# Reordering the last gate writes and the early gathers of a two-stage mixture-of-experts kernel

## Chip, cores and metric

One core of one Trainium2 chip. The metric is device time in microseconds (us) of one execution; lower is better. The kernel before was run three times: 889.64, 891.00 and 892.84 us, median 891.0 us.

## What is computed

Three layers in a row, on 3072 tokens of width 384:

```
attn:  state = w_t * state + k_t v_t ;  y_t = r_t (state + u k_t v_t)       (8 heads of 48)
moe1:  x = ((a @ w1) * (a @ w2)) @ w3 @ w_out                             (384 -> 1024 -> 384)
moe2:  noisy = x @ w_gate + log(1 + exp(x @ w_noise)) * noise              (8 experts)
       top 2 of 8, softmax weights over the two
       out += weight * (relu(x @ w1[e]) @ w2[e])    for the rows of each expert e
```

The last layer is sparse: each token goes to two of eight experts. The tokens of an expert have to be gathered, multiplied and added back to their rows of the output.

## The kernel before, in words

**Stages.** Up to about 452 us the kernel works through 24 tiles of 128 tokens, in 12 groups of two (`g`, 0 to 11). A group has 12 sub-slots (`i`, 0 to 11), and a hand-written list (`at(slot, ...)`, slot = 12 * g + i) says what is added behind which sub-slot. After the groups the eight experts run one after the other.

**Gate.** For a batch of tiles, `gate_top` (line 628) is a generator whose steps are called one at a time between other work: softplus noise, top 2, counting, expert weights (`weights`, lines 678 to 683, from the exponential of line 676), and slot numbers (lines 707 to 722). A slot is a token's place in its expert's list. `gate_put` (line 737) then writes (token, weight) pairs into the table `slots` in DRAM, 128 at a time, by an indirect DMA issued on GpSimd (POOL), line 742. The batches are of four tiles, but the last two are of two: tiles 20 and 21 (`t0` = 20), and tiles 22 and 23 (`t0` = 22), whose x is ready last. The last batch is gated while expert 0's first half already multiplies.

**An expert.** Its list has 7 tiles: 4 (`TA`) of 128 rows in the first half, 2 of 128 and one of 32 in the second (numbers 4, 5 and 6; `NT` = 7). For each tile: the index list is read from the table (SP queue, line 828 for the first experts, line 818 later), the rows of x are gathered by an indirect DMA on POOL (line 836 or 867), stored as a compact block in DRAM (SP, line 841 or 873), and read back turned by a DMA transpose into `XTx` (SP, line 848 or 879). ScalarE and VectorE split it into a high and a low part (lines 884 and 885), and TensorE multiplies: `mm1` (line 891) for eight blocks `ff` of the hidden layer, each read out by ScalarE (line 900) and VectorE (line 901), then `mm2` (line 905) for each tile, with the result scattered to the output by POOL (line 928).

**Order.** SP's DMAs are all kept in program order, and each waits in the queue for its own semaphores. VectorE, TensorE and, from the last group on, ScalarE run in program order (manual schedule); the order on POOL is that of the scheduler unless an instruction is pinned with `keep_in_program_order`. For expert 0 some gathers start before all of x or all slots are there: tile 3 (`TA` - 1) needs the slots of `t0` = 16, tile 4 (`TA`) those of `t0` = 20, and tiles 5 and 6 those of `t0` = 22. Expert 1's first half is gathered early too (lines 1037 to 1039).

**Around the change.** Behind the last group, lines 1053 to 1076 issue in this order: gate steps and `mm1(0, ff)` interleaved; in `ff` = 2 the index read of tile 4, its gather, and the turning of expert 1's first half; behind the loop the store of tile 4 (line 1067), the four writes of the last gate batch (line 1070), the turning of tile 4 (line 1073), then index reads and gathers of tiles 5 and 6 (lines 1074 to 1076), and `mm2(0, 0)` to `mm2(0, 3)`, with the stores and the turning of tiles 5 and 6 issued behind the first of them and the split `tr(0, 1)` behind the third. Expert 0's second half, `mm1(1, ff)`, follows at line 1093 and reads tiles 4 to 6 together.

Of the kernel before, what the change touches and what calls it, by code (L numbers as in the profile page):

```python
# [18 lines left out]
P = 128  # L19
# [3 lines left out]
NCH = N // P  # L23
# [8 lines left out]
TA, TB = 4, 2  # L32
# [4 lines left out]
DUMP = NT * P  # L37
# [34 lines left out]
def tile_kernel(ctx: ExitStack, tc: tile.TileContext, dt, nat, w3t, wout, w1, w2, e1, e2, cf, ci, out):  # L72
    nc = tc.nc
    pe, act, dve, pool, sp = nc.tensor, nc.scalar, nc.vector, nc.gpsimd, nc.sync
# [18 lines left out]
    x2d = nc.dram_tensor("x2_rows", [NROW, 2 * DM], U16, kind="Internal").ap()  # L93
# [376 lines left out]
    def run_todo(lo, hi):  # L470
        for slot in sorted(x for x in todo if lo <= x < hi):
            for fn, a in todo.pop(slot):
                fn(*a)
# [28 lines left out]
    for i, fn in enumerate(STEPS):  # L502
        for j in range(NCH):
            late = 3 if j == NCH - 1 and i == 1 else 0
# [93 lines left out]
    def low_p():  # L598

        while LOWP:  # L600
            l, p, h = LOWP.pop()
            dve.tensor_tensor(out=l, in0=p, in1=f(h), op=OP.subtract)

    def mo_x(g, fp):
        for tt in range(2):
            for fi in range(2):
                ff = 2 * fp + fi
                s = slice(256 * fi + P * tt, 256 * fi + P * tt + P)
                wh, wl = [W0[i][:, ff] if ff < 4 else W1[ff - 4][:, i] for i in range(2)]
                mm3(bX[tt][:, :XW], PH[g, fp][:, s], PL[g, fp][:, s], wh, wl, ff == 0, ff == 7)  # L610

    def mo_lz(g):
        for tt in range(2):
            dve.tensor_copy(out=LZ[:, 2 * g + tt, :], in_=bX[tt][:, DM:XW])

    def mo_out(g, tts=(0, 1), pin=lambda x: x):
        for tt in tts:
            t = 2 * g + tt
            xo = xos[:, 2 * DM * tt:2 * DM * tt + 2 * DM]
            pin(act.copy(out=halves(xo), in_=bX[tt][:, :DM].bitcast(U16).rearrange("p (d t) -> p t d", t=2)))  # L620
            act.dma_start(out=x2d[DUMP + t * P:DUMP + P + t * P], in_=xo)


    GB = 4
# [112 lines left out]
    def gate_put(t0, i, k):  # L737
        si, sf, SC = GT[t0]

        if t0 + GB < NCH:  # L740
            dve.tensor_copy(out=si[:, i, k:k + 1], in_=sf[:, i, k:k + 1])  # L741
        ins = pool.indirect_dma_start(out=table, out_offset=bass.IndirectOffsetOnAxis(ap=si[:, i, k:k + 1], axis=0),  # L742
                                      in_=SC[:, i, k, :], in_offset=None)
        for p in PUT:
            tc.declare_no_dep(ins.ins, p, reason="every slot is given once")
        PUT.append(ins.ins)

    def fill_table():
# [19 lines left out]
    TI, XG, RW, HM, Hh, Hl, XT = {}, {}, {}, {}, {}, {}, {}  # L768
    EP = {}

    def open_a():
        EP["a"] = ctx.enter_context(tc.tile_pool(name="epa", bufs=1))
        for hf in range(2):
            for k in "hl":
                XT[k, hf] = EP["a"].tile([P, 3, NAB[hf]], F32R, name=f"XT{k}{hf}")
        XT["x", 0] = EP["a"].tile([P, 3, NAB[0]], F32, name="XTx0")
        open_h(EP["a"], 0)
# [15 lines left out]
    def load_e(e, m, i):  # L793
        if m == 0 and e:
            rw = EP["b"].tile([P, 1536], F32, name="raww", bufs=2)
        else:
            rw = rawp.tile([P, 1538], F32, name="raw2", tag="raw64")[:, :1536]
        RW[e, m, i] = rw
        tc.keep_in_program_order(sp.dma_start(out=rw, in_=(e1, e2)[m][e, :, 1536 * i:1536 * i + 1536]))
# [31 lines left out]
    def gather_first(j, nch, e=0):  # L831
        if j < TA - 1 and not e:
            XG[e, j] = xgs[:, 2 * DM * (j % 2):2 * DM * (j % 2) + 2 * DM]
        else:
            XG[e, j] = EP["a"].tile([P, 2 * DM], U16, name="xg", bufs=NXG)
        pool.indirect_dma_start(out=XG[e, j][:rows_of(j)], out_offset=None, in_=x2d[:DUMP + nch * P],
                                in_offset=bass.IndirectOffsetOnAxis(ap=ti(e, j)[:, 0:1], axis=0))

    def store_first(j, e=0):
        w = rows_of(j)  # L840
        tc.keep_in_program_order(sp.dma_start(
            out=rows[e, 2 * TPT * j:2 * TPT * j + 2 * w].rearrange("(p t) d -> p (t d)", t=2), in_=XG[e, j][:w]))
# [15 lines left out]
    def rows_of(j):  # L858
        return TPT if j < NT - 1 else TPL

    def ti(e, j):
        hf, jj = divmod(j, TA)
        return TF[:rows_of(j), j] if e == 0 and first else TI[e, hf][:rows_of(j), jj]
# [111 lines left out]
    def gate_at(o, t0, per, put, n=GB):  # L975
        gen = gate_top(t0, n)
        for i in range(11):
            at(o + (per[i] if isinstance(per, tuple) else i // per), next, gen, None)
        for i in range(2 * n):
            at(o - o % SPG + put[i], gate_put, t0, i // 2, i % 2)  # L980


    for t0 in range(0, NCH - GB, GB):
        late = t0 == NCH - 2 * GB
        gate_at(SPG * ((t0 + GB) // 2) + 3, t0, 1 + late,
                tuple(range(8, 8 + 2 * GB)) if late else (13, 14, 17, 17, 19, 20, 23, 23))
    gate_at(SPG * (NGRP - 1) + 3, NCH - GB, (0, 0, 1, 1, 2, 3, 4, 5, 7, 7, 7), (10,) * GB, GB // 2)
    at(SPG + 2, fill_table)
    for i in range(10):
# [5 lines left out]
    for g in range(NGRP):  # L995
        if g == 2:
            ctx.enter_context(tc.manual_schedule(engines={mybir.EngineType.PE}))
        if g == NGRP - 1:
            ctx.enter_context(tc.manual_schedule(engines={mybir.EngineType.Activation}))
        sub = [(mo_ab, g, 0, 0), (mo_ab, g, 0, 1), None, (mo_ab, g, 1, 0), (mo_ab, g, 1, 1), (mo_x, g, 0),  # L1000
               (mo_ab, g, 2, 0), (mo_ab, g, 2, 1), (mo_x, g, 1), (mo_ab, g, 3, 0), (mo_ab, g, 3, 1), (mo_x, g, 2)]
        if g == 0:
            sub[:5] = [(mo_ab, g, 0, 0, bST[0]), (mo_ab, g, 1, 0, bST[1]), None, (mo_ab, g, 0, 1, bA), (mo_ab, g, 1, 1)]
        if g == NGRP - 1:
            cvx.close()
            attx.close()
            sub[8:] = [(mo_ab, g, 3, 0, PB[4]), (mo_ab, g, 3, 1, PB[5]), (mo_x, g, 1), (mo_x, g, 2)]
            open_a()
            load_e(0, 0, 0)
            load_e(0, 0, 1)  # L1010
        for i in range(12):
            if sub[i]:
                act.on = g == 0 and i < 9
                fn, *a = sub[i]
                fn(*a)
            elif g:
                mo_x(g - 1, 3)
                mo_lz(g - 1)
                mo_out(g - 1)
            k = SPG * g + i  # L1020
            run_todo(k - .5, k)
            if i not in (1, 4, 7, 10 if g < NGRP - 1 else 9):
                low_p()
            run_todo(k, k + .5)
            act.on = False
            if g == NGRP - 1:
                if i in (0, 4, 8, 10):
                    split_e(0, 0, (0, 4, 8, 10).index(i))
                if i == 10:
                    load_e(0, 1, 1)  # L1030
                if i == 0:
                    turn_first(0, TPT * (TA - 1))
                if i == 3:
                    index_first(TA - 1, 1)
                    gather_first(TA - 1, NCH - GB)
                    store_first(TA - 1)
                    index_first(0, TA, 1)
                if 4 <= i < 8:
                    gather_first(i - 4, NCH - GB, 1)
                if 5 <= i < 8:  # L1040
                    tr_first(0, TA - 1, (i - 5,))
                if i == 7:
                    turn_first(TA - 1, TPT * TA)
                    load_e(0, 1, 0)
                    for j in range(TA):
                        store_first(j, 1)
# [6 lines left out]
    t0 = NCH - GB // 2  # L1053
    gen = gate_top(t0, GB // 2)
    for ff in range(8):
        for _ in range((5, 1, 1, 0, 0)[ff] if ff < 5 else 1):
            next(gen, None)
        if ff == 0:
            mo_out(NGRP - 1, (1,), tc.keep_in_program_order)
        mm1(0, ff, (bA, bB, PB[4], PB[5]), lambda: ff == 2 and [next(gen, None) for _ in range(2)])  # L1060
        if ff == 2:
            index_first(TA, 1)
            gather_first(TA, NCH - GB // 2)
            turn_first(0, TPT * TA, 1)
        if ff >= 4:
            split_e(0, 1, ff - 4)
    store_first(TA)
    for i in range(GB // 2):
        for k in range(2):
            gate_put(t0, i, k)  # L1070
    movx.close()
    open_b()
    turn_first(TA, TPT * (TA + 1))
# [156 lines left out]
```

## Time and profile before

| | |
|---|---|
| runs | 889.64, 891.00, 892.84 us; median 891.0 |
| profiled execution | 891.74 us, of which the traced span is 889.9 us |
| TensorE matmul busy | 869.9 us (98% of the span), 7333 instructions |
| VectorE, ScalarE, GpSimd busy | 495.1, 434.6, 243.3 us |
| mean granted TensorE clock | 0.994 of full speed |
| chain that ended last | TensorE 85%, VectorE 7%, ScalarE 3%, DMA 1% |

The span is what the trace covers; the time of the execution has 1.8 us more around it. Busy shares are averages over stages: that TensorE is busy 98% says that there are few gaps, and the question is where the remaining ones lie and what ends them. In the rows below, a time in the first column is the start in us from the span's start, the next the duration; `x3` means that several were merged; a bracket gives the idle time of the engine ahead of the instruction and what ended it. `SPq` rows are DMAs being issued on the queue of SP.

### The profile page before, as it was taken

What the parts mean: (1) busy time and instruction counts of PE and PEld (TensorE: products, weight loads), DVE (VectorE), ACT (ScalarE), POOL (GpSimd) and SP (SyncE); (2) the same over time, 40 slices, a digit from 0 to 9 for tenths busy, and PEclk for the clock granted to TensorE, in tenths of its full rate; (3) what the DMA queues carried; (4) which work ended last, traced back from release to release, by engine and by line L of the source; (5) the groups of instructions that cost most, each with busy time, mean ns of one, the idle gap of its engine ahead of it and who ended that gap; (6) DMA issues with size and microseconds to landing.
All of it is one profiled execution on the core that took longest, in us unless ns stands there. A gap on an engine that the chain in (4) does not pass through costs nothing.

```text
span 889.9 us, 18271 instructions
## 1 busy us (share of the span) xinstructions
PE 869.9 (98%) x7333; PEld 809.6 (91%) x7333; DVE 495.1 (56%) x1215; ACT 434.6 (49%) x876; POOL 243.3 (27%) x216
## 2 busy tenths in 40 slices
PE   9999999999999999999999999999999999999994
PEld 6789899999999999999988989899998989999894
DVE  6899866857666667665563453443434344353320
ACT  5777566555556646644553343433344343434320
POOL 2000010131231231232343534316061341603022
PEclk9999999999999999999999999999999999999998
DMA  9964398474574654525173797929276593934113
GB/s 352 406 224 163 113 130 258 125 199 154 140 225 137 188 137 125 151 49 171 37 196 82 207 238 196 207 81 221 62 224 141 137 207 83 225 78 110 18 22 38
DMA packets 123967, 139.22 MB, mean 156 GB/s; under 512 B 74976, under 2 KB 103648, under 8 KB 123872
## 3 DMA queue, kind: packets, MB, share of 16 engines
q1 hardware_dynamic: 100336, 109.58, 43.2%
q0 software_dynamic: 12160, 19.72, 11.7%
q10 hardware_dynamic: 11376, 8.65, 3.0%
q8 instruction: 59, 0.97, 0.5%
q14 instruction: 36, 0.29, 0.1%
HBM read 88.12 MB, written 36.04 MB: 140 GB/s over the span
## 4 chain that ended last, share of the span: by engine, by line
PE 85%; DVE 7%; ACT 3%; issue 2%; DMA 1%; POOL 0%; SPq 0%; POOLq 0%; ACTq 0%; DVEq 0%
PE pb L182 25%; PE pb L183 25%; PE pb L184 25%; PE pb L332 3%; PE pb L263 3%; PE pb L923 1%; PE pb L296 1%; DVE cvz L166 1%; ACT top L153 1%; DVE am L268 1%; PE pb L520 1%; PE pb L412 1%; DVE fg L210 1%; DVE w3l L173 0%; DVE WAl L173 0%
## 5 line engine op out<-in xcount | busy, mean ns | idle before, releaser
L928 POOL DMA_INDIRECT out<-ye,ti x49 | 77.7, 1585 | 225.7 <-ACT ye L918 205.2
L182 PE MATMUL pb<-XTh,WAh 128*128 128x512 f32 (+1 forms) x384 | 132.5, 345 | 1.6 <-ACT XTh L884 1.6
L184 PE MATMUL pb<-XTh,WAl 128*128 128x512 f32 (+1 forms) x384 | 132.1, 344 | 0.0
L183 PE MATMUL pb<-XTl,WAh 128*128 128x512 f32 (+1 forms) x384 | 131.8, 343 | 0.1
L901 DVE SCALAR_TENSOR_TENSOR HH<-pb,HH 128x256 fp32r<-128x256 f32 (+1 forms) x128 | 71.0, 557 | 105.6 <-ACT HH L900 101.3
L182 PE MATMUL pb<-WBh,HH 128*128 128x384 f32 x384 | 129.3, 337 | 0.0
L183 PE MATMUL pb<-WBl,HH 128*128 128x384 f32 x384 | 128.5, 335 | 0.0
L184 PE MATMUL pb<-WBh,HH 128*128 128x384 f32 x384 | 128.4, 334 | 0.0
L900 ACT ACTIVATE HH<-pb 128x256 fp32r<-128x256 f32 (+1 forms) x128 | 62.7, 492 | 109.9 <-PE pb L184 105.3
L918 ACT ACTIVATE ye<-pb,ti 128x384 f32<-128x384 f32 x42 | 24.4, 582 | 130.3 <-PE pb L184 101.8
L742 POOL DMA_INDIRECT slots<-g_sc,g_si x48 | 51.8, 1078 | 125.4 <-DVE g_si L741 73.1
L183 PE MATMUL pb<-xl,WAh 128*128 128x256 f32 x288 | 80.9, 281 | 0.8 <-DVE xl L339 0.8
L182 PE MATMUL pb<-xh,WAh 128*128 128x256 f32 x288 | 81.5, 284 | 0.0
L182 PEld LDWEIGHTS pb<-XTh,WAh 128*128 128x128 f32 x384 | 72.7, 189 | 9.7 <-ACT XTh L884 1.9
L183 PE MATMUL pb<-xl,WBh 128*128 128x256 f32 x288 | 81.0, 281 | 0.0
L182 PE MATMUL pb<-xh,WBh 128*128 128x256 f32 x288 | 81.0, 281 | 0.0
L184 PE MATMUL pb<-xh,WBl 128*128 128x256 f32 x288 | 81.0, 281 | 0.0
L184 PE MATMUL pb<-xh,WAl 128*128 128x256 f32 x288 | 80.8, 281 | 0.0
L183 PEld LDWEIGHTS pb<-XTl,WAh 128*128 128x128 f32 x384 | 73.0, 190 | 7.9 <-DVE XTl L885 0.3
L184 PEld LDWEIGHTS pb<-XTh,WAl 128*128 128x128 f32 x384 | 72.8, 190 | 7.6
L182 PEld LDWEIGHTS pb<-WBh,HH 128*128 128x128 f32 x384 | 72.1, 188 | 5.0 <-ACT WAh L806 3.8
L243 POOL TENSOR_TENSOR rku<-nrk 128x384 f32<-128x384 f32 x21 | 21.6, 1031 | 194.5 <-DVE cc L250 78.9
(203 smaller groups left out, 2064.4 us busy)
## 6 DMA issues: line engine op xcount, KB each, us to landing
dtc<-dt SPq DMA_DIRECT2D x24, 772.0 KB
raw<-e SPq DMA_DIRECT2D x18, 768.0 KB
raww<-e SPq DMA_DIRECT2D x14, 768.0 KB
nrk<-nat SPq DMA_DIRECT2D x24, 384.0 KB
expert_rows<-xg SPq DMA_DIRECT2D x45, 192.0 KB
rawf<-w3t SPq DMA_DIRECT2D x16, 512.0 KB
nv<-nat SPq DMA_DIRECT2D x24, 256.0 KB
out<-zeros SPq DMA_DIRECT2D x9, 576.0 KB
```

The source lines that it names most:

```text
L153: act.activation(out=t.bitcast(F16).rearrange("p (n t) -> p n t", t=2)[:, :, 1], in_=top, func=AF.Copy)
L182: pin(pe.matmul(o, wh, xh, start=start, stop=False))
L183: pe.matmul(o, wh, xl, start=False, stop=False)
L184: pe.matmul(o, wl, xh, start=False, stop=stop)
L243: on.tensor_tensor(out=t, in0=RK[j][:, :DM], in1=RK[j][:, DM:], op=OP.mult)
L263: pe.matmul(bST[hb][:, P * a:P * a + P], KT[j][q, a].rearrange("p s i -> p (s i)"), RT[j][q, a].rearrange("p s i -> p (s i)"), start=True, ...
L332: pe.matmul(o, lt, rh, start=st, stop=en, tile_position=tp)
L742: ins = pool.indirect_dma_start(out=table, out_offset=bass.IndirectOffsetOnAxis(ap=si[:, i, k:k + 1], axis=0), in_=SC[:, i, k, :], in_offs ...
L900: act.activation(out=Hh[hf][:, ff], in_=bank[:, :n], func=AF.Relu)
L901: dve.scalar_tensor_tensor(Hl[hf][:, ff], bank[:, :n], 0.0, f(Hh[hf][:, ff]), op0=OP.max, op1=OP.subtract)
L918: act.activation(out=y[:n], in_=bank[:n], func=AF.Copy, scale=wt)
L928: ins = pool.indirect_dma_start(out=out, out_offset=bass.IndirectOffsetOnAxis(ap=ti(e, j)[:, 0:1], axis=0), in_=y[:n], in_offset=None, com ...
```

## The change

It does four things. The last gate batch: the two generator steps with the exponential and the weights are called ahead of `mm1(0, 0)` in place of ahead of `mm1(0, 1)` and `mm1(0, 2)`, and so ahead of the first block's read-out on ScalarE and VectorE. Its four slot writes are issued ahead of tile 4's gather on POOL, and both are pinned there, as are the gathers of tiles 5 and 6; tile 4's gather and store move behind the writes. The last four slot writes of `t0` = 16 are issued in sub-slots 0, 0, 1, 1 of the last group in place of 0, 1, 2, 3. The index reads of tile 3 and of expert 1, tile 3's gather and store move from sub-slot 3 to 1 of the last group, and expert 1's four gathers from sub-slots 4 to 7 to sub-slots 2 to 5.

```diff
@@ gate_put
             tc.declare_no_dep(ins.ins, p, reason="every slot is given once")
+        if t0 + GB > NCH:
+            tc.keep_in_program_order(ins)
         PUT.append(ins.ins)
@@ gather_first
-        pool.indirect_dma_start(out=XG[e, j][:rows_of(j)], out_offset=None, in_=x2d[:DUMP + nch * P],
-                                in_offset=bass.IndirectOffsetOnAxis(ap=ti(e, j)[:, 0:1], axis=0))
+        ins = pool.indirect_dma_start(out=XG[e, j][:rows_of(j)], out_offset=None, in_=x2d[:DUMP + nch * P],
+                                      in_offset=bass.IndirectOffsetOnAxis(ap=ti(e, j)[:, 0:1], axis=0))
+        if j >= TA:
+            tc.keep_in_program_order(ins)
@@ the list of slots
-                tuple(range(8, 8 + 2 * GB)) if late else (13, 14, 17, 17, 19, 20, 23, 23))
+                (8, 9, 10, 11, 12, 12, 13, 13) if late else (13, 14, 17, 17, 19, 20, 23, 23))
@@ the last group
-                if i == 3:
+                if i == 1:
                     index_first(TA - 1, 1)
                     gather_first(TA - 1, NCH - GB)
                     store_first(TA - 1)
                     index_first(0, TA, 1)
-                if 4 <= i < 8:
-                    gather_first(i - 4, NCH - GB, 1)
+                if 2 <= i < 6:
+                    gather_first(i - 2, NCH - GB, 1)
@@ behind the last group
     for ff in range(8):
-        for _ in range((5, 1, 1, 0, 0)[ff] if ff < 5 else 1):
+        for _ in range(7 if ff == 0 else ff > 4):
             next(gen, None)
...
         if ff == 2:
             index_first(TA, 1)
-            gather_first(TA, NCH - GB // 2)
             turn_first(0, TPT * TA, 1)
         if ff >= 4:
             split_e(0, 1, ff - 4)
-    store_first(TA)
     for i in range(GB // 2):
         for k in range(2):
             gate_put(t0, i, k)
+    gather_first(TA, NCH - GB // 2)
+    store_first(TA)
     movx.close()
     open_b()
     turn_first(TA, TPT * (TA + 1))
```

## Rows read from the trace of the kernel before

**Rows 1.** Timeline of TensorE, 486 to 494 us: around its longest wait.

```profile
486.93 0.34 PE L184 MATMUL pb<-WBh,HH 128*128 128x384 f32 x1
488.87 0.40 PE L182 MATMUL pb<-XTh,WAh 128*128 128x288 f32 x1 [1.60 <-ACT XTh L884]
489.36 0.40 PE L183 MATMUL pb<-XTl,WAh 128*128 128x288 f32 x1
...
490.18 0.44 PE L182 MATMUL pb<-XTh,WAh 128*128 128x288 f32 x1
...
493.30 0.37 PE L183 MATMUL pb<-XTl,WAh 128*128 128x288 f32 x1
```

**Rows 2.** Busy time of each engine by stretch, then PEclk, DMA share, GB/s.

```profile
491.00:492.00 1.00, 1.00 (x6) 1.00 (x5) 0.44 (x2) 0.38 (x1) 0.79 (x1) 0.50 1.00 399
```

**Rows 3.** Waits of TensorE, 440 to 520 us (all there are): total, times, longest.

```profile
PE pb L182 <- ACT XTh L884: 1.6, 1, 1.6
PE pb L727 <- DVE g_rb L714: 0.2, 1, 0.2
```

**Rows 4.** Timeline of SP's DMA queue, 469 to 487 us.

```profile
469.06 0.35 SPq L841 DMA_DIRECT2D expert_rows<-xg  x1
471.35 1.21 SPq L848 DMA_TRANSPOSE XTx<-expert_rows  x1
476.28 0.81 SPq L828 DMA_DIRECT2D tf<-slots  x2
482.32 1.02 SPq L841 DMA_DIRECT2D expert_rows<-xg  x2
484.94 2.09 SPq L848 DMA_TRANSPOSE XTx<-expert_rows  x1
```

**Rows 5.** Waits of SP's queue, 455 to 500 us: total, times, longest.

```profile
SPq L828 <- DMA slots<-g_sc,g_si: 10.8, 2, 7.2
```

**Rows 6.** Timeline of POOL, 465 to 481 us.

```profile
465.38 0.97 POOL L836 DMA_INDIRECT xg<-x_rows,tf  x1 [8.86 <-issue]
466.66 1.55 POOL L742 DMA_INDIRECT slots<-g_sc,g_si  x1 [0.30 <-DVE HH L901]
...
469.78 1.71 POOL L742 DMA_INDIRECT slots<-g_sc,g_si  x1 [0.30 <-issue]
471.79 1.16 POOL L742 DMA_INDIRECT slots<-g_sc,g_si  x1 [0.30 <-issue]
479.28 0.98 POOL L836 DMA_INDIRECT xg<-x_rows,tf  x1 [6.33 <-DMA tf<-slots]
```

**Rows 7.** Timeline of ScalarE, 458 to 462 us.

```profile
458.44 0.80 ACT L620 COPY xos<-pb 128x768 uint16<-128x768 uint16 x1
...
459.65 0.60 ACT L900 ACTIVATE HH<-pb 128x512 fp32r<-128x512 f32 x1 [0.40 <-PE pb L695]
461.07 0.20 ACT L676 ACTIVATE g_d<-g_d 128x2 f32<-128x2 f32 x1 [0.82 <-DVE g_d L675]
```

**Rows 8.** Timeline of VectorE, 459 to 467 us.

```profile
459.19 0.36 DVE L669 TENSOR_TENSOR g_cm<-g_cm,g_mb 128x8 bf16<-128x8 bf16 x2
460.28 0.69 DVE L901 SCALAR_TENSOR_TENSOR HH<-pb,HH 128x512 fp32r<-128x512 f32 x1 [0.72 <-ACT HH L900]
...
463.21 0.16 DVE L707 TENSOR_TENSOR g_ct<-pb,g_gap 128x8 f32<-128x8 f32 x1
...
464.54 0.17 DVE L722 CAST g_si<-g_sf 128x4 int32<-128x4 f32 x1
464.62 1.88 DVE L901 SCALAR_TENSOR_TENSOR HH<-pb,HH 128x512 fp32r<-128x512 f32 x3
```

**Rows 9.** Timeline of TensorE: the first matmul of the fifth block.

```profile
461.61 0.39 PE L182 MATMUL pb<-XTh,WAh 128*128 128x512 f32 x1
```

**Rows 10.** Slot writes, line 742: ns min/median/max; the page's group with their mean.

```profile
L742 POOL DMA_INDIRECT slots<-g_sc,g_si x48: 952/995/1705, 175.8 to 471.8; - x48
L742 POOL DMA_INDIRECT slots<-g_sc,g_si x48 | 51.8, 1078 | 125.4 <-DVE g_si L741 73.1
```

## The prediction

> **What bounds the kernel now.** TensorE is almost never idle, so I first looked for the places where it is. In the stretch that the change touches, its timeline shows one long gap [rows 1]: the last matmul of expert 0's first half starts at 486.93, the next one, the first of the second half, at 488.87 after 1.60 us of waiting for the split of `XTx`, and the second of the half again waits, 0.49 behind the first. Then TensorE is slow: from 490.18 to 493.30, 13 matmuls of 0.24 us, and the stretch in between has a granted clock of 0.50 [rows 2], that is 1.2 in place of 2.4 GHz. What TensorE did before the clock fell was to wait. So this place costs 1.60 of idle, 0.37 of the second matmul (0.49 less 0.12, half of 0.24), and 1.56 (half of 3.12) of slow clock: 3.5 us. The list of TensorE's waits from 440 to 520 holds one more entry, 0.2 us for the gate [rows 3]. Nothing else there can be won.
>
> What the 1.60 us wait for is followed back along SP's queue [rows 4]: the turning of tiles 5 and 6 at 484.94, their stores at 482.32, and at 476.28 the reads of their index lists. From that issue to TensorE's restart at 488.87 it takes 12.6 us. The index read waits for the slot writes to land (the longest such wait is 7.2 us [rows 5]), and the last of them leaves POOL at 472.95. On POOL [rows 6] the four writes run from 466.66, behind tile 4's gather at 465.38, which had stood idle for 8.86 us for its own index list. So the change cuts at the right chain. The question is what holds the index read when the writes no longer do.
>
> **The last weights ahead of the first read-out.** In program order ScalarE now meets the exponential of the gate before its copy of x (line 620) and before the read-outs. Before, the copy began at 458.44, and the exponential, of 0.20, came behind the first read-out [rows 7]. The exponential needs VectorE's step behind the counts, which end at 459.55 [rows 8]; with 0.16 for that step, as for the gate's like ones, it ends near 459.9. So the copy now starts about 1.4 later, and all that is queued behind it does too: the write of x to DRAM (read first by the gather of tiles 5 and 6, some 18 us later, so worth nothing) and the first block's read-out, which followed the copy by 1.21 (459.65) and now comes near 461.1. VectorE's part follows 0.63 behind (460.28) and takes 0.69, so the first block's bank is free near 462.4. The fifth block uses the same bank and began at 461.61 [rows 9]: a new wait of 0.8 us. Against it the gate's matmul need no longer wait its 0.2 [rows 3]. TensorE is 0.6 late at the end of the first half, and the gap at 487 hides that, as it is 1.97 long; without that cover it would cost 0.6.
>
> The slot numbers: the second read-out on VectorE now ends near 462.9, and the last steps (463.21 to 464.71 before) begin there, so they are ready at 464.4 instead of 464.71, and the first write starts at 464.7, with POOL's gap of 0.30, instead of 466.66 [rows 6].
>
> **The writes ahead of tile 4's gather.** The writes come 2.0 us sooner. But the gather of tile 4 now comes behind them, and behind it on SP stand, in order, its store, its turning, and only then the index reads of tiles 5 and 6. Before, store and turning were issued at 469.06 and 471.35 [rows 4], while the writes were still going out, and were free. Now they are in the chain. Its sum, with d for a slot write's time on POOL:
>
> - first write at 464.7, four writes of d + 0.30;
> - tile 4's gather, 0.97 on POOL; from its end to the store's issue 2.06 (480.26 to 482.32, quiet) or 2.71 (466.35 to 469.06, with expert 1's turning beside it). I take 2.06, since that turning is now earlier;
> - store to turning 2.29 (469.06 to 471.35), turning 1.21 to issue; then the index read.
>
> That is 472.4 + 4d. The median write takes 0.995, the shortest 0.952, the longest 1.705, the mean 1.078 [rows 10]. Of the last four, three took 1.55, 1.71 and 1.16 [rows 6], so I take the mean, not the median: index read at 476.74, against 476.28. The shortest gives 476.2, the longest 479.2, and 2.71 in place of 2.06 adds 0.65. A gain larger than 0.1 is excluded as long as SP's queue keeps its order. The landing of the writes is no longer what comes last: the last leaves POOL near 470, and even the 3.33 us that the index read stood behind the last write before end at 473.3.
>
> **Weighed against a rule.** The gather at 465.38 took 0.97, hardly the shortest time, although VectorE ran read-outs with two tensor inputs beside it from 464.62 [rows 8]. The Trainium skill, page GPSIMD Engine Reference, section Specifications, says that GpSimd shares its SBUF interface with VectorE and contends with VectorE's instructions of two SBUF inputs. By that rule all four writes would be long, since VectorE's read-outs and splits now fall on each of them; by the row they need not be. The long case is a rival below, with its price from the rows.
>
> **Early gathers.** Two index reads, five gathers and a store move two sub-slots up on SP and POOL, with two VectorE casts of the `t0` = 16 writes. TensorE waits for none of this before or after [rows 3], and in program order they pass nothing else on either queue. Worth nothing by itself; if the cover is gone the bound is below 0.2, the only other wait. It clears DMA work of expert 1 out of the way of the last writes, which is why I took 2.06. Tile 4's index also comes sooner, but its gather is now behind the writes anyway. The pins cost no instruction.
>
> **Sum.** The index read is 0.5 later, and so are the gathers, stores, turning and TensorE's restart, each of which only hangs on it. TensorE itself is 0.6 late, so its wait is about as long as before, and I leave the slow clock stretch as it is. Profiled execution: 891.74 + 0.5 = 892.2. That execution stands 0.7 above the median of the runs, 891.0, so in terms of the median: 891.5. A measurement of this kernel tells 0.3% (2.7 us) from no change.
>
> **Rivals.** Times in terms of the median.
>
> - The wait goes: the index read follows the writes' landing near 473.3, three us sooner, and everything is there before TensorE. It gains 3.5 and pays 0.6: 888.1, faster by 0.33%. For it: the writes do come sooner. Against: this needs SP to pass tile 4's turning, and its rows stand in program order, each behind its wait. Chance 0.10.
> - Slower: VectorE holds up the slot writes. At d = 1.705 the index read comes at 479.2 and the time is 894.0; over 0.3% it decides from d = 1.63. For it: two of the last four were that long. Against: the gather of 0.97, the mean. Chance 0.17.
> - The clock does not fall, as the wait is split between 462 and 488: 1.56 less, 889.9. Against: the long wait hardly shrinks. Chance 0.08.
> - The change doesn't do what it says: the scheduler's order on POOL leaves gather or scatter ahead of the writes, and the index read is as before: 891.0. The pins speak against it. Chance 0.05.
> - The forecast, 891.5: 0.60.
>
> **How the numbers follow.** Range: from the shortest chain with the slow clock gone, 891.0 - 1.6 = 889.4, to the longest writes, 894.0; outside lie the first rival and the second with the late landing, together under 0.2. Faster by over 0.3%: most of the first rival and a little scatter, 0.08. Slower: most of the second and of its sum with a longer slow stretch, 0.16. Within: 0.76.
>
> **What would show it.** Right: the slot writes start near 464.7; tile 4's gather behind them near 470; SP's index reads directly behind the turning of tile 4, near 476.7, with no wait for slots; a wait of 0.8 before the fifth block; a wait of 1.5 to 2 and a slow stretch near 488. Wrong: an index read by 474, no wait ahead of the second half, no stretch of 0.50 clock; or slot writes of 1.6 each; or a new TensorE wait elsewhere.

## The result, and the profile after

The changed kernel takes 898.58 us (median of 6 runs, 896.29 to 899.71); the kernel before, run beside it, 891.92 (6 runs, 889.64 to 895.82). The ratio on record is 1.0069, with a 95% interval of [1.0042, 1.0097] (here and below it is not the quotient of the two medians): slower, by more than the 0.3% of which the prediction speaks, and outside the range of the forecast.

The profiled execution of the changed kernel took 898.66 us, 6.92 more than that of before. The page shows a TensorE that works hardly longer (871.4 us of matmul in place of 869.9) in a span 7.0 longer: most of the time went into waiting.

```profile
PE 871.4 (97%) x7333; PEld 811.1 (90%) x7333; DVE 496.2 (55%) x1215; ACT 434.1 (48%) x876; POOL 241.7 (27%) x216
```

TensorE's waits of the changed kernel from 440 to 520 us (total, times, longest), against [rows 3]:

```profile
PE pb L182 <- ACT XTh L888: 6.5, 1, 6.5
```

The 0.2 for the gate is gone as predicted, no new wait has come between 455 and 489, and the one wait ahead of expert 0's second half has grown from 1.60 to 6.46. To see where the 6.92 us are, I mark two instructions in each execution: expert 0's first matmul (A), and the first matmul of its second half (R). TensorE's timeline, changed kernel, answering to [rows 1]:

```profile
455.75 0.39 PE L182 MATMUL pb<-XTh,WAh 128*128 128x512 f32 x1
...
488.95 0.34 PE L184 MATMUL pb<-WBh,HH 128*128 128x384 f32 x1
495.74 0.61 PE L182 MATMUL pb<-XTh,WAh 128*128 128x288 f32 x1 [6.46 <-ACT XTh L888]
```

and, kernel before, the one row that [rows 1] does not hold:

```profile
452.88 0.39 PE L182 MATMUL pb<-XTh,WAh 128*128 128x512 f32 x1
```

- Up to A: 455.75 against 452.88, 2.87 later. The change issues hardly anything there, and the next two fences show where more than half of it comes from.
- From A to R: 39.99 against 35.99 us, 4.00 more. This is the change.
- From R to the end of the span: 401.12 against 401.08. Nothing.

The first part shows how a difference of two profiles can mislead. Matched matmul by matmul, the changed kernel is 1.2 us behind at 22 us and 2.8 behind at 40. The busy time by stretch (length; TensorE, weight load, VectorE, ScalarE, POOL with their instructions; granted clock, DMA share, GB/s) from 28 to 36 us, ahead of everything that was changed, before:

```profile
28.00:36.00 8.00, 7.00 (x44) 6.15 (x45) 7.57 (x19) 6.03 (x15) 0.00 (x0) 1.00 1.02 409
```

and changed:

```profile
28.00:36.00 8.00, 6.83 (x33) 6.03 (x33) 7.48 (x18) 5.06 (x11) 0.00 (x0) 0.79 1.02 409
```

The same code ran at a granted clock of 0.79 there: 33 matmuls were done in place of 44. In a second profile of the same changed kernel, told of below, this stretch has 1.00 again and A lies at 453.22. A second profile of the kernel before has A at 453.19. So the 2.87 of the 6.92 is this execution's chance, while the 4.00 from A to R is there again (41.18 against 35.99).

SP's queue in the changed kernel, answering to [rows 4]:

```profile
465.06 0.34 SPq L830 DMA_DIRECT2D tf<-slots  x1
477.48 0.35 SPq L845 DMA_DIRECT2D expert_rows<-xg  x1
479.41 1.22 SPq L852 DMA_TRANSPOSE XTx<-expert_rows  x1
480.80 0.92 SPq L830 DMA_DIRECT2D tf<-slots  x2
487.18 2.05 SPq L845 DMA_DIRECT2D expert_rows<-xg  x2
492.04 1.26 SPq L852 DMA_TRANSPOSE XTx<-expert_rows  x1
```

Store, turning, and the index read directly behind it: the order that the prediction named. POOL, answering to [rows 6]:

```profile
467.54 0.96 POOL L742 DMA_INDIRECT slots<-g_sc,g_si  x1 [8.30 <-DMA tf<-slots]
...
471.33 1.71 POOL L742 DMA_INDIRECT slots<-g_sc,g_si  x1 [0.30 <-issue]
473.34 1.18 POOL L838 DMA_INDIRECT xg<-x_rows,tf  x1 [0.30 <-issue]
483.71 0.96 POOL L838 DMA_INDIRECT xg<-x_rows,tf  x1 [9.19 <-DMA tf<-slots]
484.97 0.87 POOL L838 DMA_INDIRECT xg<-x_rows,tf  x1 [0.31 <-issue]
486.15 1.66 POOL L932 DMA_INDIRECT out<-ye,tf  x1 [0.30 <-issue]
488.12 1.59 POOL L932 DMA_INDIRECT out<-ye,tf  x1 [0.30 <-issue]
```

Two things are new. The first slot write waits 8.30 us for `tf<-slots`, the landing of tile 4's index read, and not for VectorE. And behind the gathers of tiles 5 and 6 stand two scatters of the first half's results, where before there was one. The chain of waits (start, length, what) runs through them:

```profile
484.97 3.90 DMA xg<-x_rows,tf
...
488.88 3.10 DMA expert_rows<-xg
...
492.04 3.19 DMA XTx<-expert_rows
```

Before, the store of the last tile took 1.89, and the turning 3.43:

```profile
482.99 1.89 DMA expert_rows<-xg
...
484.94 3.43 DMA XTx<-expert_rows
```

### The profile page after: what moved, and what is told of

It is laid out like the page before. It is cut to its first block, busy times and chain, and to the rows that moved or that the text cites. A ratio compares the mean times of both kernels' runs of the same rounds, so it can differ in the third digit from the quotient of the medians.

```text
span 896.9 us, 18270 instructions
## 1 busy us (share of the span) xinstructions
PE 871.4 (97%) x7333; PEld 811.1 (90%) x7333; DVE 496.2 (55%) x1215; ACT 434.1 (48%) x876; POOL 241.7 (27%) x216
## 4 chain that ended last, share of the span: by engine, by line
PE 83%; DVE 6%; DMA 4%; issue 2%; ACT 2%; POOL 2%; SPq 0%; POOLq 0%; DVEq 0%; ACTq 0%
PE pb L182 25%; PE pb L183 24%; PE pb L184 24%; PE pb L332 3%; PE pb L263 3%; DMA xg<-x_rows,tf 1%; PE pb L927 1%; PE pb L296 1%; DVE cvz L166 1%; POOL slots L742 1%; DMA slots<-g_sc,g_si 1%; DMA rawf<-wout 1%; DMA expert_rows<-xg 1%; POOL xg L838 1%; ACT top L153 0%
## 5 line engine op out<-in xcount | busy, mean ns | idle before, releaser
L905 DVE SCALAR_TENSOR_TENSOR HH<-pb,HH 128x256 fp32r<-128x256 f32 (+1 forms) x128 | 71.1, 557 | 104.4 <-ACT HH L904 99.5
```

The lines of the kernel that those rows point to most:

```text
L905: dve.scalar_tensor_tensor(Hl[hf][:, ff], bank[:, :n], 0.0, f(Hh[hf][:, ff]), op0=OP.max, op1=OP.subtract)
```

## The experiments

Three theories were set against each other. **A, the place in the queue:** tile 4's gather, store and turning now stand between the slot writes and the index reads of tiles 5 and 6, and that alone makes the wait. **B, the other parts:** the early weights, or the early gathers of expert 1, cost the time. **C, the collision:** since the chain is late, the scatters of the first half meet the last gathers and stores on the DMA engines and stretch them. "Wait" is the wait ahead of the second half in the one profiled execution of each kernel.

**1. The place alone, undone and done.** The changed kernel with only tile 4's gather and store put back ahead of the writes:

```diff
         if ff == 2:
             index_first(TA, 1)
+            gather_first(TA, NCH - GB // 2)
...
+    store_first(TA)
     for i in range(GB // 2):
         for k in range(2):
             gate_put(t0, i, k)
-    gather_first(TA, NCH - GB // 2)
-    store_first(TA)
```

> The changed kernel, but with tile 4's gather and store back ahead of the last four slot writes; early weights, early gathers and pins stay. Theory A (tile 4's store and turning now stand on SP's queue ahead of the index reads of tiles 5 and 6, behind a gather that comes later): TensorE's wait ahead of the second half falls from 6.5 to 2 us or less, and from the first matmul of expert 0 to the first one of its second half it takes 35 to 36.3 us (36.0 before, 40.0 after); ratio to the kernel before 0.997 to 1.002. Rival B (the early weights and the early gathers cost the time): the wait stays over 4 us, the stretch near 40, the ratio near 1.007.

Measured: 891.09 us against 892.85; 0.9997 [0.9973, 1.0022]. The wait is 3.52 and A to R 37.05, more than A's figures, which I had taken from the one profile of before. The profiled execution was one of the slower ones of this kernel (892.86, ninth of 12).

The kernel before with only that move and the pins of the diff:

```diff
-            gather_first(TA, NCH - GB // 2)
...
-    store_first(TA)
     for i in range(GB // 2):
         for k in range(2):
             gate_put(t0, i, k)
+    gather_first(TA, NCH - GB // 2)
+    store_first(TA)
```

> The kernel before, with only tile 4's gather and store moved behind the last four slot writes (and the pins). Theory A: the wait is 5 to 7 us, the stretch from expert 0's first matmul to its second half 39 to 40.5 us, ratio 1.004 to 1.009. Rival B: the wait stays near 1.6, the stretch near 36, the ratio 0.998 to 1.002.

Measured: 896.72 against 892.85; 1.0046 [1.0021, 1.0071]. The wait, 9.04, and A to R, 42.57, are more than A's figures. TensorE's timeline:

```profile
496.20 0.61 PE L182 MATMUL pb<-XTh,WAh 128*128 128x288 f32 x1 [9.04 <-ACT XTh L888]
```

The whole loss goes with this one move: undone, the kernel is where before is; done alone, it is slow. B is left with little.

**2. The other parts by themselves.** The early weights alone:

```diff
-        for _ in range((5, 1, 1, 0, 0)[ff] if ff < 5 else 1):
+        for _ in range(7 if ff == 0 else ff > 4):
```

> The kernel before, with only the early weights (all seven gate steps ahead of the first block's multiplication). Theory A: nothing to gain or lose, as the slot writes stand behind tile 4's gather; ratio 0.998 to 1.002, the wait ahead of the second half 1.5 to 4 us as in the runs with the order of before, and no new wait of TensorE ahead of the fifth block. The step of the prediction (a new wait of 0.8 us near the fifth block) would show as a second TensorE wait of 0.5 to 0.9 us. Rival B: ratio 1.003 or more.

Measured: 1.0009 [0.9985, 1.0033], wait 3.65, and no second wait of TensorE. The early gathers alone (the new list of slots, `i == 1`, `2 <= i < 6`):

> The kernel before, with only the earlier slot writes of tiles 16 to 19 and the earlier index reads and gathers in the last group. Theory A: tile 4's index read comes up to 2 us sooner, counted from expert 0's first matmul; the time is within 0.997 to 1.001. Rival B: ratio 1.003 or more, with a wait over 4 us.

Measured: 0.9982 [0.9957, 1.0006], wait 4.12; tile 4's index read came 2.2 us sooner after A (7.60 in place of 9.76; 8.98 in the second profile of before). Both intervals hold 1: B has fallen. Both waits are above the 1.60 of before, but each belongs to its own execution: those profiled took 895.90 and 894.38, among the slowest of their kernels, with medians of 894.05 and 891.11.

**3. The queue place without giving up the early writes.** If A is right, the index reads and gathers of tiles 5 and 6 need only go ahead of tile 4's store and turning on SP:

```diff
     gather_first(TA, NCH - GB // 2)
+    for j in (NT - 2, NT - 1):
+        index_first(j, 1)
+        gather_first(j, NCH)
     store_first(TA)
     movx.close()
     open_b()
     turn_first(TA, TPT * (TA + 1))
-    for j in (NT - 2, NT - 1):
-        index_first(j, 1)
-        gather_first(j, NCH)
```

> The changed kernel, with the index reads and gathers of tiles 5 and 6 issued ahead of the store and the turning of tile 4 on SP. Theory A: the index read waits for the slot writes alone and comes some 3 to 4 us sooner than in the changed kernel, the wait falls to 0 to 2.5 us, the stretch to 34 to 36.5; ratio 0.996 to 1.001. Rival B: the wait stays over 4 us, ratio near 1.007. Theory C (the two scatters ahead of the stores are what costs most): the wait falls by less than 2 us.

Measured: 889.35 against 892.85; 0.9974 [0.9953, 0.9995]: faster than before, and, by the ratios, 0.9974 against 1.0069 and (experiment 5) 1.0054, 0.8% to 0.9% faster than the changed kernel. SP's queue shows the index read 20.2 us behind A (453.24 here), where the changed kernel has 25.05:

```profile
473.40 0.81 SPq L830 DMA_DIRECT2D tf<-slots  x2
476.24 0.36 SPq L845 DMA_DIRECT2D expert_rows<-xg  x1
478.23 1.23 SPq L852 DMA_TRANSPOSE XTx<-expert_rows  x1
```

and TensorE waits 1.45:

```profile
488.22 0.40 PE L182 MATMUL pb<-XTh,WAh 128*128 128x288 f32 x1 [1.45 <-ACT XTh L888]
```

**4. The scatters.** The changed kernel, with the scatters of the first half held back and issued behind the gathers of expert 1's second half (line 928 before):

```diff
+        if HELD is None: scatter()
+        else: HELD.append(scatter)
...
     need(1, 1, 0)
+    with tc.issue_after(GL[0]):
+        for fn in held: fn()
```

> The changed kernel, with the scatters of expert 0's first half issued on POOL behind the gathers of expert 1's second half, so that none runs beside the gathers and stores of tiles 5 and 6. Theory C (the two scatters that now run there slow the gather, the store and the turning): the turning of tiles 5 and 6 follows its stores by 2 us in place of 3.1, and the wait falls from 6.5 to 3.5 to 4.5 us; ratio 1.002 to 1.005. Theory A alone (place in the queue, without collision): the wait stays at 6 us or more, ratio 1.006 to 1.008.

Measured: 895.45 against 892.85; 1.0028 [1.0006, 1.0051], wait 4.12 in place of 6.46. Its chain of waits:

```profile
482.80 2.50 DMA xg<-x_rows,tf
...
485.31 2.46 DMA expert_rows<-xg
...
487.84 3.40 DMA XTx<-expert_rows
```

The three legs of the last tile (gather to store, store to turning, turning to landing) are 8.4 us here and 10.2 in the changed kernel. So C is a part of the loss: 0.28% is left of the 0.69% and (experiment 5) 0.54%, which is about half, and the intervals are too wide to say it closer. The place in the queue is left, and with it the rest; moving it takes the whole loss away with the scatters where they were (experiments 1 and 3).

Both repairs, this and that of experiment 3, together:

> The changed kernel with both repairs: index reads and gathers of tiles 5 and 6 ahead of tile 4's store and turning, and the scatters of the first half behind the gathers of expert 1's second half. Theories A and C together: the turning follows the stores by about 2 us, XTx is there before TensorE is, the wait is under 1 us and the clock does not fall; from first matmul to second half 34.2 to 35 us, ratio 0.993 to 0.997. Theory A alone: as the run with the index read ahead, wait 1 to 2 us, ratio 0.996 to 0.999.

Measured: 889.39 against 892.09; 0.9972 [0.9954, 0.999], wait 1.09. No better than the first repair alone.

**5. The changed kernel once more**, for a second profile:

> The changed kernel once more, for the size of the loss. Its profile had 4.0 us of 6.9 between expert 0's first matmul and its second half, and 2.9 us ahead of that, in loading and folding the weights, where the two kernels have the same instructions. If the 2.9 us are chance of that execution, the first matmul comes at 453 to 455 us and the ratio is 1.004 to 1.006; if they belong to the change, it comes after 455.5 again and the ratio is 1.007 or more.

Measured: 897.58 against 892.09; 1.0054 [1.0034, 1.0073]. A at 453.22, the stretch from 28 to 36 at full clock (the row above had 0.79), wait 7.65:

```profile
28.00:36.00 8.00, 6.80 (x44) 5.75 (x43) 7.66 (x17) 6.02 (x14) 0.00 (x0) 1.00 1.03 412
```

```profile
494.41 0.61 PE L182 MATMUL pb<-XTh,WAh 128*128 128x288 f32 x1 [7.65 <-ACT XTh L888]
```

**6. What holds the first slot write.** In the changed kernel it waits for the read of tile 4's index list, since both touch the table, and the write comes behind the read in program order. The rows that tile 4 reads were all written before, by the batch `t0` = 20, so the order is not needed. The version of both repairs, with it dropped:

```diff
+            for p in IX4:
+                tc.declare_no_dep(ins.ins, p, reason="tile 4's slots are all given before")
```

> The run with both repairs, and the last slot writes no longer ordered behind the index read of tile 4 (which reads rows of the table that they never write). If the writes wait for that read's landing and not for their slot numbers, the first write comes near 9.8 us after expert 0's first matmul in place of 11.8 (the numbers are ready at 9.5), the index reads of tiles 5 and 6 near 16.5 to 17.5 in place of 18.5, TensorE's wait is gone, and the ratio to before is 0.994 to 0.997. If the numbers or POOL set the writes, nothing moves and the wait stays near 1.1.

Measured: 888.17 against 890.73; 0.9977 [0.9961, 0.9993]. The first write now hangs on VectorE's slot numbers:

```profile
464.52 0.96 POOL L742 DMA_INDIRECT slots<-g_sc,g_si  x1 [6.25 <-DVE g_si L722]
```

That is 9.85 us behind A, 1.9 sooner than in the changed kernel. But the index read comes 19.6 behind A, later than I expected:

```profile
465.47 4.52 SPq L857 DMA_TRANSPOSE XTx<-expert_rows  x1
474.27 0.81 SPq L832 DMA_DIRECT2D tf<-slots  x2
```

Its chain of waits names what is late next, the landing of the writes:

```profile
468.76 5.42 DMA slots<-g_sc,g_si
```

Beside them expert 1's turning runs. TensorE's wait is down to 0.38, so there is nothing left to win here; this is the lowest median of all (the three repairs' intervals overlap, so I don't rank them).

**7. How steady the kernel before is.** Experiments 1 and 2 left kernels that are as fast as before with waits of 3.5 to 4.1. Before with its scatters held back, and before unchanged, each profiled:

> The kernel before with the scatters of the first half behind the gathers of expert 1's second half, and nothing else. Theory C: even with the one scatter of before, store and turning of tiles 5 and 6 are slowed in most executions; the turning follows the last store by about 2 us, the wait is 1 to 2.5 us in place of 3.5 to 4, ratio 0.997 to 1.000. Without the collision in before: no change, 0.999 to 1.001.

Measured: 889.48 against 890.73; 0.9983 [0.9965, 1.0002], wait 3.35. The last store still took 3.4 to the turning, without any scatter beside it, so C's expectation for the kernel before is missed. SP's queue:

```profile
482.34 0.90 SPq L841 DMA_DIRECT2D expert_rows<-xg  x2
486.29 1.27 SPq L848 DMA_TRANSPOSE XTx<-expert_rows  x1
```

and the DMA view of 483 to 487 us (packets, MB, share of 16 engines) has one packet of instruction code in that stretch:

```profile
q8 instruction: 1, 0.02, 2.2%
```

It runs from 483.80 to 485.20, and the store, whose other packets had all started by 484.15, stands still beside it. The DMA view from 484.15 to 485.15, and from 485.15 to 485.60:

```profile
DMA packets 0, 0.00 MB, mean 0 GB/s; under 512 B 0, under 2 KB 0, under 8 KB 0
```

```profile
q1 hardware_dynamic: 3, 0.00, 5.2%
```

The store's last three packets start from 485.19 on, as the packet of code ends. Each of the thirteen profiles has one such packet (16 KB, 0.96 to 1.60 us) between the index read of tiles 5 and 6 and R, 30.5 to 32.7 us behind A, in whatever order the chain runs. Where it starts within the last store (experiments 1, first part, 2, 3 and 7), store to turning takes 2.8 to 3.6. Where it lies elsewhere it is 1.6 to 1.9 (before, before again, experiment 1, second part, both repairs, experiment 6), except in experiment 4, where it starts just ahead of the store (2.5), and in the two profiles of the changed kernel, where a second scatter runs beside the store (3.2 and 3.5). No run moves the packet, so this is read from the traces alone.

> The kernel before once more, for the spread of its profile: the runs with its order (gather back, weights alone, early gathers alone) waited 3.5 to 4.1 us ahead of the second half, the profiled execution of before 1.6. If that one was a favourable execution, this one waits 2.5 to 4.5 us and the stretch from first matmul to second half is 36.5 to 38.

Measured: one run, 888.62 us; wait 0.51, A to R 34.04. My expectation is missed, to the other side. The index reads:

```profile
473.55 0.93 SPq L828 DMA_DIRECT2D tf<-slots  x2
```

20.36 us behind A, where the first profile of before has 23.41. So two profiles of one kernel have A to R 35.99 and 34.04, and its 35 runs in one comparison reach from 888.4 to 897.0. The kernel before lives with this wait on the edge. In both of its profiles the packet of code starts behind the last store, in the other four of its order within it: this is a part of what moves the wait, and the index read's own place, 20.4 to 23.4 behind A, is the other, whose cause is not settled.

A to R over all profiles, in us, with the time of the profiled execution; A to R is the sum of the two columns before it:

| order on POOL and SP | execution | A to index read | index read to R | A to R |
|---|---|---|---|---|
| kernel before, two profiles | 891.74, 888.62 | 23.41, 20.36 | 12.59, 13.68 | 35.99, 34.04 |
| tile 4's gather ahead of the writes, other edits (experiments 1, 2, 2, 7) | 892.86, 895.90, 894.38, 892.90 | 22.95, 23.36, 22.44, 22.52 | 14.10, 13.81, 15.21, 14.36 | 37.05, 37.18, 37.66, 36.88 |
| gather behind the writes (changed, changed again, experiment 1) | 898.66, 898.23, 898.94 | 25.05, 26.00, 27.99 | 14.95, 15.18, 14.58 | 39.99, 41.18, 42.57 |
| the same, scatters late (4) | 895.48 | 24.79 | 12.87 | 37.66 |
| index reads ahead of tile 4's store (3, 4, 6) | 889.52, 891.06, 889.96 | 20.16, 18.48, 19.60 | 14.81, 16.14, 14.31 | 34.98, 34.62, 33.91 |

Most of these executions are among the slower ones of their kernel, so the table is to be read by its groups and not by the medians. The six profiles with the gather ahead of the writes have the index read at 22.5 in the mean and R 14.0 behind it; the two of the changed kernel 25.5 and 15.1. So of 4.1 us in the mean, 3.0 are the later index read, which is theory A, and 1.1 the longer way from there. Experiment 4 keeps the late index read, 24.8, and shortens the way to 12.9, so that holding the scatters back gains more than the later chain had lost there.

The two profiles of the changed kernel and the two of before differ by 5.6 from A to R in the mean (40.6 less 35.0) and by 1.2 behind it (401.5 less 400.3, the slow clock): 6.8, where the medians differ by 6.7 and 5.5.

## Why the prediction was wrong

The forecast was 0.5 us of loss from one late index read. By its own steps, in us behind A (the prediction's A is 452.88):

| step | before | before again | predicted | changed | changed again |
|---|---|---|---|---|---|
| first slot write | 13.8 | 12.7 | 11.8 | 11.8 | 12.1 |
| tile 4's gather | 12.5 | 11.4 | 17.3 | 17.6 | 18.8 |
| its store | 16.2 | 15.4 | 20.4 | 21.7 | 22.7 |
| its turning | 18.5 | 19.0 | 22.7 | 23.7 | 24.6 |
| index read of tiles 5, 6 | 23.4 | 20.4 | 23.9 | 25.1 | 26.0 |
| their turning | 32.1 | 29.6 | 32.5 | 36.3 | 37.4 |
| R | 36.0 | 34.0 | 36.5 | 40.0 | 41.2 |

Between the first profiles of the two kernels, the 4.00 us are 0.45 that were predicted, 1.2 of the index read's place that were mis-sized, and 2.6 from the index read to the turning of tiles 5 and 6; from there to R it is 0.2 less than before.

- **The step that failed** is the sentence of the sum that "so are the gathers, stores, turning and TensorE's restart, each of which only hangs on it". It takes the way from the index read to R, 12.6 us in one profile, as a fixed length behind a read that comes 0.5 later. They hang on the index read, but they also share the DMA engines with whatever runs at that time. The way took 14.95 in the changed kernel, and of all thirteen profiles the 12.59 is the shortest: the five others with the gather ahead of the writes have 13.7 to 15.2. Between the first two profiles two legs make the difference. The last tile's gather took 3.90 (2.42 before): the packet of code runs beside it from 486.60 to 487.83, the gather's other packets with data have all started by 487.0, and its last one starts at 487.82. The DMA view of the changed kernel from 487.80 to 488.00 holds that one packet:

```profile
q0 software_dynamic: 1, 0.00, 10.4%
```

  The store behind it took 3.10 (1.89 before), and beside it runs a second scatter of the first half: TensorE's work does not wait for the chain, so a chain that starts later meets traffic that it used to precede. Experiment 4 takes the scatters away, and the three legs together fall from 10.2 and 10.4 (changed, changed again) to 8.4. The number of scatters alone does not order the profiles: with one, the legs are 7.8 and 7.9 (before, twice), 8.8 to 9.3 (experiments 1, first part, 2 and 3); with two, 9.9 in experiment 1, second part; with none, 8.9 in experiment 7 and 9.9 in both versions of experiments 4 and 6 that have the index reads ahead, where the packet of code falls into the turning, which takes 4.9 and 5.1. By the Trainium skill, page DMA: Bandwidth & Descriptors, section Issuing engines are not separate DMA queues, transfers started by SP and by GpSimd run on the same 16 engines and interleave; experiment 4, which moved only POOL's issues and shortened SP's store from 3.10 to 2.46, agrees.
- **The index read's place** is the other failure, and over all profiles the larger one. The prediction had it 0.5 behind that of before; the changed kernel has it at 25.1 and 26.0, 1.7 and 2.6 behind the 23.4 of the profile that the prediction used. That one was late for its order, as the other five have 20.4 to 23.4: by the means it is 3.0.
- **The term that was mis-sized** is tile 4's gather to its store. I had 2.71 and 2.06 from two rows and took the shorter, since expert 1's turning would be out of the way. It was: SP issued it at 465.63, and the DMA view from 474.5 to 477.5 holds next to nothing but the gather's own packets. Yet the store came 2.96 behind a gather that itself took 1.18 in place of 0.97. The two are 1.1 of the 1.2. So it was not the turning that set the longer price, and what did is open; in the four profiles with the gather behind the writes and SP's order kept, the store comes 2.6 to 3.4 behind the gather's end.
- **The slot writes.** Right in their place, by luck. The slot numbers were ready at 9.5 behind A, 2.0 sooner than I had them (464.4, or 11.5), because the copy of the logits that the gate starts from was late in the one profile of before. VectorE's timeline, before and changed:

```profile
454.97 0.17 DVE L614 COPY LZ<-pb 128x16 f32<-128x16 f32 x1 [2.64 <-remote]
```

```profile
455.96 0.17 DVE L614 COPY LZ<-pb 128x16 f32<-128x16 f32 x1 [0.92 <-PE pb L184]
```

  2.09 behind A there, 0.21 here, and 0.2 in the eleven other profiles. What I had not seen is the order against tile 4's index read, which held the write to 11.8 in spite of it. The diff did not show it; the rule for it was in the code, where orders that aren't needed are declared away one by one.
- **Their duration:** 0.96, 0.96, 0.96 and 1.71, a mean of 1.15 with 1.08 taken. In the second profile of the changed kernel they are 1.69, 0.96, 1.71 and 1.16, a mean of 1.38, which by the prediction's own 4d is 1.2 us more. So the slower rival, for which 1.63 was needed, came about in part there. What makes a write long stands in the traces. VectorE around the long write of the changed kernel, which began at 471.33:

```profile
471.25 0.95 DVE L811 TENSOR_TENSOR WBl<-raw,WBh 128x768 fp32r<-128x768 f32 x1
472.12 0.68 DVE L905 SCALAR_TENSOR_TENSOR HH<-pb,HH 128x512 fp32r<-128x512 f32 x1
```

  It began within a split of the weights, whose two inputs lie in SBUF, and ended 0.92 after the next instruction of VectorE had begun. Of the 624 slot writes of the thirteen profiles, 218 took over 1.03 us, and every one of these began while VectorE ran a `TENSOR_TENSOR` with both inputs in SBUF, of 128 columns or more. Read-outs (L905), which have one input in PSUM, never did this: the four writes that began within one took 0.96. So the row that the prediction weighed against the rule, the 0.97 of the gather at 465.38 beside read-outs, could not test it. With the rule of the Trainium skill's page GPSIMD Engine Reference, section Specifications, which names VectorE's instructions of two SBUF inputs, the traces agree; but a write was long only when it began within such an instruction, so not all four were.
- **The new wait of 0.8 before the fifth block** didn't come, since the gate ran 1.9 sooner than I had it; nor did TensorE's lateness of 0.6. The first half's last matmul came 33.20 behind A, with 34.05 before. **The early gathers and the early weights** are worth nothing, as predicted: 0.9982 and 1.0009, both intervals with 1 inside.
- **The rivals.** The slower rival had the sign, but its cause, the long writes, made only 0.3 and 1.2 us in the two profiles. The faster one, "the wait goes", was turned down because it needs SP to pass tile 4's turning. Experiment 3 gives it just that, and its index read at 473.40 stands where that rival put it, 473.3: the reason for which it was turned down was right. Its gain of 0.33% lies in the interval, although the wait shrank to 1.45 there and did not go.
- **The slow clock.** I left it as it was, for a wait of the same length. It follows the wait: granted clock 0.66 from 490 to 495 in before, after the wait of 1.60, and 1.00 there after 1.45 in experiment 3; in the changed kernel 0.51 from 495 to 500, after 6.46. Windows of before, of experiment 3 and of the changed kernel:

```profile
490.00:495.00 5.00, 5.00 (x29) 5.00 (x28) 1.09 (x5) 1.12 (x3) 4.09 (x4) 0.66 0.99 367
```

```profile
490.00:495.00 5.00, 5.00 (x40) 5.00 (x39) 2.09 (x8) 1.71 (x5) 3.89 (x4) 1.00 0.90 329
```

```profile
495.00:500.00 5.00, 4.26 (x17) 4.05 (x18) 1.72 (x5) 1.96 (x5) 3.03 (x3) 0.51 0.90 314
```

  The four profiles with waits of 1.45 or less end 399.5 to 399.6 behind R; all others, from 1.60 up, 400.5 to 402.0. Between the first profile of before and that of experiment 3, with waits of 1.60 and 1.45, that is 1.6 us behind R, ten times the difference of the waits.
- **Two readings of the rows.** The 7.2 us of [rows 5] is the wait of tile 4's index read; that of tiles 5 and 6 is the other of the two, 3.6. And [rows 6] gives "issue" for the 8.86 us ahead of tile 4's gather, not its index list. Neither enters the sum.

## What to carry to other kernels

When a step is moved behind another on one queue, write down everything that stands behind it on the next queue: here a gather moved by one place on POOL drew a store and a turning into the chain on SP, and putting the late reads ahead of them turned a loss of 0.5% to 0.7% into a gain of 0.3%. A chain that starts later does not shift as a whole: price its transfers by what runs at the new time, and where two rows of one transfer differ and the reason is only guessed, let the longer one into the sum. Take a second profile of the kernel before ahead of any sum in single microseconds: here two of them differ by 2 us in the very stretch, the price taken from the first was the shortest of thirteen, and two fifths of the difference between the first two profiles lay where hardly anything had been changed.

## What was not expected of the hardware

- The same code at the program's start, 28 to 36 us, ran at a granted clock of 1.00 in one profile of the changed kernel and at 0.79 in another, and A lay at 453.22 and 455.75. Of the thirteen profiles two have 0.79 there, the other being that of both repairs together (A at 455.04). The clock is not all that moves A, though: of the eleven with 1.00, ten have A between 452.88 and 454.66, and one, that of the early weights, at 455.22.
- A store of 48 KB took 1.54 to 3.54 us until its turning was released, and the turning of tiles 5 and 6 landed after 3.1 to 6.0, in orders that differ little; one packet of instruction code, or a second scatter, beside them goes with the long ones: the stores of 2.5 and more, the turnings of over 3.4. Beside the longest turning (experiment 1, second part) a scatter took 6.1 to land.
- The last slot write of experiment 6, 128 pairs of 8 bytes, took 5.42 us from its start on POOL to what waited for its landing, or 4.5 from POOL's end (it ran 0.96), with a turning issued from 465.47 to 469.99 beside it. In the profile of before the index read came 3.33 behind POOL's end [rows 4, 6].
- A slot write issued on GpSimd takes 0.95 to 1.03 us by itself, and what is left of a VectorE split with two SBUF inputs, plus 0.83 to 0.96, when it begins within one (31 writes).
